# Hashed attention with experts: the later pairs' hash in four products, and the joining work two tiles back

## The chip, the cores and the metric

The kernel runs on one core of a Trainium2 chip. The metric is device time in microseconds of one execution, the median of the runs shown. Engines are called TensorE (PE), VectorE (DVE), ScalarE (ACT), GpSimd (POOL) and SyncE (SP, which here only issues DMAs). "PEld" is TensorE's weight load, "SPq" the queue of SyncE.

## The reference

Three layers follow each other; only the first is touched by the change.

```python
# attention: 2 batches, 8 heads, 768 tokens, 64 columns a head
q_bits = (q @ proj > 0); k_bits = (k @ proj > 0)          # proj: 64 x 6
q_bucket = sum(q_bits * 2 ** arange(6)); k_bucket likewise
scores = where(q_bucket == k_bucket, q @ k.T / 8, -1e9)   # token by token
attn = softmax(scores); x = attn @ v                      # f32
# mixture of 8 experts: each token goes to the expert of its largest x @ w_gate,
# is scaled by a gate weight and a sigmoid, runs through relu(x @ w1) @ w2
# last layer: elu(x @ w_in) @ w_out
```

Everything is f32. The kernel gets f32 accuracy from products of the type fp32r by splitting an operand into a high part (the rounded copy, "hi") and a low part (operand minus hi, "lo") and adding the products of the parts.

## The kernel before

**Attention** takes 16 heads as 8 pairs. A head has 6 tiles of 128 query tokens, so a pair has 12 tiles and there are 96 tiles, n = 0 to 95; "tile s of a pair" is n modulo 12. A head has two halves of 384 tokens, which have numbers m = 0 to 31 (three tiles each). One loop over n (lines 884 to 935) writes each engine's instructions in this order; every engine works through its own list in order and waits by semaphores. In the turn of tile n the list holds:

- `stage_M(n-1)`: VectorE takes the maximum of the scores of the tile before (L333), GpSimd makes from it a factor and a bias (L334, L335);
- `stage_A(n)`: sums on GpSimd that are due (L388);
- `early`: what an earlier turn has put off to here;
- `stage_T(n-3)`: TensorE turns the exponentials (six transposes, L362), ScalarE copies them out as hi (L364), VectorE makes lo (L365);
- `late[0]`, the first step of preparing the next pair;
- `stage_S(n)`: TensorE's scores, two column halves with two products each: L314 (q hi and lo with k hi), and L315, the masked product: q hi with k lo, and 38 mask rows that add a large negative number where the buckets differ;
- `stage_R` of a half, if due; `stage_V`, four products with v (L378);
- `stage_E(n-1)`: ScalarE's exponential (L342), which frees the score buffer (there are two);
- `stage_O` at the end of a half: ScalarE copies the output out; and `late[1]`, the second step of preparing.

**Preparing the next pair** is done in tiles 1, 2, 4, 5 (transposes of q and k, L203, copies and low parts) and 7, 8: the hash. `prep_Z(pr, j)` for j = 0, 1 (a column half of 384 tokens) issues six products (L229): q with a 128x128 matrix that holds proj for both heads, as hi x hi, hi x lo and lo x hi, and k likewise, into one PSUM buffer. In the following turn's `late[1]`, at its end, VectorE compares all 128 rows with 0 and multiplies with a column of amplitudes (`prep_Ze`, L245), which gives the rows of the mask for both heads. After j = 1, `restack` (L266) has SyncE move rows by DMA into the operands `kb` and `qb` of the next pair's heads: two for `kb` and one for `qb` for each head. The first pair's hash takes a way of its own (`first_Ze`). Transposes, hash and joins share three PSUM buffers of tag "t" (`ps_t`), which go round.

**The joining work.** Outputs leave PSUM as hi part and lo part products in 128 rows. `stage_O(m)`, at n = 3m+8, copies them to SBUF (L407), and a DMA shifts one half of the rows over (L408); the sum is put on a list with the tile 3m+11 at which `stage_A` runs it (L388). Copy and shift target are two tiles `o2` and `o1` of the pool `raw_p`, which has six large buffers of tag "w"; they are free again after the sum. From m = 26 on another way is taken. The same six buffers take the pieces of the experts' weights, 512 KB each: `load_piece` issues the first four at tiles 72, 75, 78 and 81 (L107), and they stay until attention is over. Once the second head of a pair has its half, `stage_R(m)`, here called the join, at n = 3m+13, multiplies the outputs of both heads with a matrix of the identity and the gates' weights (L454, six matmul records), which turns them to tokens by columns; its VectorE part (L462, L481) runs in the next turn's `early`. The output tiles `osb` have two buffers.

In the middle pairs the second head's halves are m = 2 and 3 (modulo 4), so joins stand in tiles 7 and 10 of the following pair; in pairs 3 and 7 the halves go by turns, m = 1 and 3 (modulo 4).

After attention come the gates' last part, the experts (a stretch in which TensorE is full) and the last layer; all wait for attention's end.

Of the kernel before, what the change touches and what calls it, by code (L numbers as in the profile page):

```python
# [8 lines left out]
F32 = mybir.dt.float32  # L9
F32R = mybir.dt.float32r  # L10
BF16 = mybir.dt.bfloat16
I32 = mybir.dt.int32
AF = mybir.ActivationFunctionType
ALU = mybir.AluOpType
# [5 lines left out]
BIG = float(2.0 ** 98)  # L20
NBITS = 6
# [4 lines left out]
def kernel(  # L26
# [15 lines left out]
    nc = tc.nc  # L42
    B, H, S, D = q.shape
# [5 lines left out]
    HALF = 3  # L49
    HC = HALF * 128  # L50
# [38 lines left out]
    raw_p = ctx.enter_context(tc.tile_pool(name="raw", bufs=6))  # L89
# [5 lines left out]
    PW = KD * F // 4  # L95
# [16 lines left out]
    ap2 = att.enter_context(tc.tile_pool(name="ap2", bufs=2))  # L112
    ops_s = ctx.enter_context(ExitStack())
    ap1 = ops_s.enter_context(tc.tile_pool(name="ap1", bufs=1))
    ps_s = att.enter_context(tc.tile_pool(name="ps_s", bufs=2, space=PSUM))
    ps_t = att.enter_context(tc.tile_pool(name="ps_t", bufs=3, space=PSUM))
# [45 lines left out]
        nc.gpsimd.memset(opnd[st, "kb"][64:96].bitcast(F32), -BIG)  # L162

    constant_rows(1)
    bdf, bdh, bdl = (ap1.tile([128, 2, 128], t, name="bd" + x) for x, t in (("f", F32), ("h", F32R), ("l", F32R)))
    nc.vector.memset(bdf, 0.0)
    for hh in range(2):
        rows = slice(64 * hh, 64 * hh + 64)
        src = pj[rows, None, :].to_broadcast([64, 2, NBITS])
        for nm, g0, c0, step in ((0, 32 * hh, 0, NBITS), (1, 64, NBITS * hh, 32)):  # L170
            dst = bdf[rows, nm, g0:g0 + 2 * step].rearrange("p (r c) -> p r c", r=2)[:, :, c0:c0 + NBITS]
            nc.scalar.activation(dst, src, AF.Copy)
    nc.scalar.activation(bdh, bdf, AF.Copy)
    nc.vector.tensor_tensor(bdl, bdf, bdh, ALU.subtract)
    bd = {nm: (bdh[:, i], bdl[:, i]) for i, nm in enumerate("qk")}
    amp = ap1.tile([128, 1], F32, name="amp")
    thr = ap1.tile([128, 1], F32, name="thr")
# [8 lines left out]
    for hh in range(2):  # L186
        p0 = 64 * hh
        rows, idc = slice(p0, p0 + 64), ident[p0:p0 + 64, None, p0:p0 + 64]
        nc.gpsimd.tensor_copy(rw[rows, :, hh, 0:D], idc.to_broadcast([64, H // 2, D]))
        nc.gpsimd.tensor_copy(rw_end[rows, :, 0:D], idc.to_broadcast([64, 2, D]))  # L190
    nc.gpsimd.memset(zt0, 0.0)

    hl = {}
# [26 lines left out]
    zt = {}  # L220
    zps = {}

    def prep_Zm(pr, j, nm):
        sl = slice(j * HC, (j + 1) * HC)
        if nm == "q":
            zps[pr, j] = ps_t.tile([128, HC], F32, tag="t", name="zps")
        hi, lo = hl[pr, nm]
        for i, (w, m) in enumerate(((bd[nm][0], hi), (bd[nm][0], lo), (bd[nm][1], hi))):
            nc.tensor.matmul(  # L229
                zps[pr, j], w, m[:, sl], start=(nm == "q" and i == 0), stop=(nm == "k" and i == 2)  # L230
            )
# [10 lines left out]
    def prep_Ze(pr, j):  # L242
        if j == 0:
            zt[pr] = ap2.tile([128, S], F32R, tag="z", name="z", bufs=1)
        nc.vector.tensor_scalar(  # L245
            zt[pr][:, j * HC:(j + 1) * HC], zps.pop((pr, j)), 0.0, amp[:, 0:1], ALU.is_gt, ALU.mult
        )

    def prep_Z(pr, j):
        prep_Zm(pr, j, "q")  # L250
        prep_Zm(pr, j, "k")

        def evac():
            prep_Ze(pr, j)
            if j == 1 and pr:
                restack(pr, "z")

        return (lambda: None), evac

    def restack(pr, what, heads=(0, 1)):  # L260
        for hh in heads:
            st = 2 * (pr % 2) + hh
            r0 = 64 * hh

            def cp(dst, p0, src, s0, n):
                nc.sync.dma_start(  # L266
                    opnd[st, dst][p0:p0 + n].bitcast(F32), src[s0:s0 + n].bitcast(F32)
                )

            if what == "q":  # L270
                hi, lo = hl[pr, "q"]
                cp("qa", 0, hi, r0, 64)
                cp("qa", 64, lo, r0, 64)
                cp("qb", 0, hi, r0, 64)
            elif what == "k":
                hi, lo = hl[pr, "k"]
                cp("ka", 0, hi, r0, 64)
                cp("ka", 64, hi, r0, 64)
                cp("kb", 0, lo, r0, 64)
            else:  # L280
                cp("kb", 64, zt[pr], (64, 96 + NBITS)[hh], NBITS)
                cp("kb", 96, zt[pr], (96, 64 + NBITS)[hh], NBITS)
                cp("qb", 64, zt[pr], 32 * hh, 2 * NBITS)

    vst = {}

# [103 lines left out]
    def stage_O(m):  # L390
        hd, hf = part_of(m)
        pr, hh = divmod(hd, 2)
        r0 = 64 * hh
        ps = ops.pop(m)
        if pr == NPAIR - 1 or hh == 0:
            t = ap2.tile([128, HC], F32, tag="osb", name="osb", bufs=2)
            osb.setdefault((pr, hf), []).append(t)
        if pr == NPAIR - 1:
            nc.scalar.activation(t, ps, AF.Copy)  # L399
            return  # L400
        t = osb[pr, hf][0][r0:r0 + 64]
        if m >= NM - 6:
            nc.scalar.activation(t, ps[0:64], AF.Copy)
            early.append(lambda: nc.vector.tensor_tensor(t, ps[64:128], t, ALU.add))
        else:
            w, u = (raw_p.tile([128, PW], F32, tag="w", name=x)[:, 0:HC] for x in ("o2", "o1"))
            nc.scalar.activation(w, ps, AF.Copy)  # L407
            nc.sync.dma_start(u[r0:r0 + 64], w[64 - r0:128 - r0])  # L408
            add.append((3 * m + 11, t, w[r0:r0 + 64], u[r0:r0 + 64]))

    rinv = {}
    sums_m = {}
# [24 lines left out]
    def stage_R(m):  # L437
        hd, hf = part_of(m)
        pr, hh = divmod(hd, 2)
        if hh == 0:  # L440
            return lambda: None
        b, pp = divmod(pr, H // 2)
        if pp == 0:
            xw[b, hf] = xlast if 2 * b + hf == NG - 1 else x_p.tile(
                [128, HALF, XC], F32, tag="xw", name="xw", bufs=NG - 1
            )
            nc.gpsimd.memset(xw[b, hf][:, :, DM:], 0.0)
            lg[b, hf] = x_p.tile([128, HALF, 2, 2 * E], F32, tag="lg", name="lg", bufs=NG)
        ts = osb.pop((pr, hf))
        ps = small_psum([128, HALF, 2, RW], False)  # L450
        for i, t in enumerate(ts):
            for a in range(HALF):
                o, w = (ps[:, a, i, :], rw_end[:, i, :]) if len(ts) == 2 else (ps[:, a], rw[:, pp])
                nc.tensor.matmul(o, t[:, a * 128:(a + 1) * 128], w, start=True, stop=True)  # L454
        return lambda: evac_R(pr, hf, ps)
# [427 lines left out]
    for n in range(NQ + 3):  # L883
        pr, s = divmod(n, 2 * NC)
        nx = pr + 1
        if NQ - 24 <= n < NQ - 12 and n % 3 == 0:
            load_piece((n - NQ + 24) // 3)
        if 1 <= n < NQ + 1:
            stage_M(n - 1)
        stage_A(n)  # L890
        both(early)
        early = []
        if 3 <= n < NQ + 3:
            m, part = divmod(n - 5, HALF)
            stage_T(n - 3, (lambda: stage_G2(m)) if m >= 0 and part == 0 else None)
        m, part = divmod(n - 4, HALF)
        if 0 <= m < NM and part == 0:
            stage_G(m)
        if late:
            late[0]()  # L900
        if n < NQ:
            stage_S(n)
        m, part = divmod(n - 13, HALF)
        if 0 <= m < NM - 3 and part == 0:
            early.append(stage_R(m))
        if n == NQ:
            stage_R(NM - 3)()
        m, part = divmod(n - 6, HALF)
        if 0 <= m < NM:
            stage_V(m, part)  # L910
        if 1 <= n < NQ + 1:
            stage_E(n - 1)
        if 0 <= m < NM and part == HALF - 1:
            stage_O(m)
        if late:
            late[1]()
            late = []
        for f, a in todo.pop(n, ()):
            f(*a)
        if n == NQ:  # L920
            ops_s.close()
            m2a = ctx.enter_context(tc.tile_pool(name="m2a", bufs=1, side="right", reuse_waits="tile"))
            split_piece(0, nc.gpsimd, nc.gpsimd, rest0)
            xt0 = [raw_p.tile([128, KD * CAP], F32R, tag="w", name="xt0") for _ in range(2)]
        if nx < NPAIR:
            if s % 3 and s < 9:
                late = prep(nx, s // 3 * 2 + s % 3 - 1)
            if s in v_at:
                i = v_at.index(s)
                early.append(lambda a=(nx, i // 3, i % 3): prep_V(*a))  # L930
            if nx + 1 < NPAIR:
                if s == 6:
                    load_pair(nx + 1, "qk")
                elif s == 11:
                    load_pair(nx + 1, "v")
# [423 lines left out]
```

## Time and profile before

| | |
|---|---|
| median of 3 runs | 722.96 us (722.31 to 724.34) |
| profiled execution | 723.3 us, span 721.5 us |
| granted clock, mean | 0.993 |
| TensorE busy | 704.7 us (98%) |
| VectorE busy | 553.6 us (77%) |
| ScalarE busy | 422.7 us (59%) |
| GpSimd busy | 206.0 us (29%) |

The profile is of one execution. The span runs from the first to the last instruction; the time of the execution is 1.8 us longer. A busy matmul is not one at its peak, since matmuls overlap and their ends are modelled: two matmuls with rows of 0.34 us each can follow each other at 0.17 us. Times in all rows count from the span's start.

### The profile page before, as it was taken

The numbers are of one execution on the slowest core, as the hardware profiler recorded it, in microseconds if no ns is written. First come the engines' busy times: TensorE is split into PE (matmuls) and PEld (weight loads), VectorE is DVE, ScalarE is ACT, GpSimd is POOL, SyncE is SP. The second block draws the span as 40 slices with busy tenths as digits, with TensorE's granted clock in tenths as the row PEclk, the third lists the DMA queues.
The fourth block names the chain that finished last, engine by engine and source line by source line (L and its number), as shares of the span: only waits on it lengthen the run. The fifth ranks groups of instructions, "written<-read, shape, count | busy, mean of one in ns | idle before, by whom it ended". The sixth has DMA issues, their size and how long they took to land.

```text
span 721.5 us, 12243 instructions
## 1 busy us (share of the span) xinstructions
PE 704.7 (98%) x4239; PEld 633.3 (88%) x4240; DVE 553.6 (77%) x1045; ACT 422.7 (59%) x843; POOL 206.0 (29%) x491
## 2 busy tenths in 40 slices
PE   6999999999999999999999999999999999999996
PEld 4899999999999988999999999788888888888885
DVE  5888988989898988788888887977688546934333
ACT  3887978879788875666666675444543224422221
POOL 7445454455545554112352241000000000002012
PEclk9899999999999999999999999999999999999999
DMA  8747576585773137987889786332122000001011
GB/s 192 181 104 172 163 184 173 129 213 137 167 218 98 76 105 224 291 251 222 260 241 251 203 230 191 103 102 84 63 88 87 31 0 2 1 0 59 0 59 61
DMA packets 108532, 97.69 MB, mean 135 GB/s; under 512 B 33416, under 2 KB 94472, under 8 KB 108464
## 3 DMA queue, kind: packets, MB, share of 16 engines
q1 hardware_dynamic: 106000, 90.44, 46.8%
q0 software_dynamic: 2304, 6.40, 2.4%
q8 instruction: 35, 0.57, 0.3%
q14 instruction: 33, 0.27, 0.1%
q10 hardware_dynamic: 160, 0.00, 0.0%
HBM read 64.15 MB, written 10.72 MB: 104 GB/s over the span
## 4 chain that ended last, share of the span: by engine, by line
PE 52%; issue 32%; DMA 7%; ACT 3%; DVE 2%; POOL 1%; SPq 1%; POOLq 0%; ACTq 0%; DVEq 0%
PE hps L1059 12%; PE o L378 8%; PE yps L1072 8%; PE t L362 7%; DMA out_dram<-part,tidt 5%; PE s L314 4%; PE s L315 4%; PE yps L1074 3%; PE zps L229 2%; PE sp L454 2%; ACT p L342 1%; PE prep L203 1%; PE xTp L1041 1%; DMA qb<-qhi 1%; DVE ptlo L365 1%
## 5 line engine op out<-in xcount | busy, mean ns | idle before, releaser
L365 DVE TENSOR_TENSOR ptlo<-t,pthi 128x384 fp32r<-128x384 f32 x192 | 100.1, 549 | 26.7 <-ACT pthi L364 24.5
L342 ACT ACTIVATE p<-s,bi,sc 128x768 f32<-128x768 f32 x96 | 96.1, 1001 | 21.4 <-POOL bi L335 20.0
L364 ACT ACTIVATE pthi<-t 128x384 fp32r<-128x384 f32 x192 | 84.9, 498 | 24.6 <-PE t L362 23.7
L765 DVE TENSOR_TENSOR wl<-wraw,wh 128x1024 fp32r<-128x1024 f32 x63 | 77.3, 1229 | 21.8 <-ACT wh L762 19.6
L333 DVE TENSOR_REDUCE nm<-s 128x1 f32<-128x768 f32 x96 | 91.0, 948 | 0.3 <-POOL vst L293 0.3
L1211 POOL DMA_INDIRECT out_dram<-part,tidt x12 | 11.5, 962 | 263.5 <-DVE part L1208 262.2
L1173 ACT ACTIVATE ee<-gps 128x512 f32<-128x512 f32 x48 | 28.7, 599 | 97.9 <-PE gps L1163 97.9
L1072 PE MATMUL yps<-h,wh 128*128 128x448 f32 x256 | 84.4, 380 | 0.0
L362 PE MATMUL t<-ident,p 128*128 128x128 f32 x576 | 80.5, 275 | 1.6 <-DVE qlo L212 1.6
L314 PE MATMUL s<-ka,qa 128*128 128x384 f32 x192 | 74.3, 387 | 3.0 <-ACT p L342 2.6
L1163 PE MATMUL gps<-x2h,vl 128*128 128x512 f32 x192 | 75.9, 395 | 0.0
L1193 PE MATMUL a<-vh,gh 128*128 128x512 f32 x192 | 75.6, 394 | 0.0
L1193 PE MATMUL a<-vh,gl 128*128 128x512 f32 x192 | 75.4, 393 | 0.0
L1163 PE MATMUL gps<-x2h,vh 128*128 128x512 f32 x192 | 75.3, 392 | 0.0
L1163 PE MATMUL gps<-x2l,vh 128*128 128x512 f32 x192 | 75.2, 392 | 0.0
L1193 PE MATMUL a<-vl,gh 128*128 128x512 f32 x192 | 74.9, 390 | 0.0
L362 PEld LDWEIGHTS t<-ident,p 128*128 128x128 f32 x576 | 68.5, 142 | 5.2 <-DVE qlo L212 2.0
L1174 DVE TENSOR_SCALAR ee<-ee 128x512 f32<-128x512 f32 x48 | 20.4, 425 | 66.2 <-ACT ee L1173 66.2
L1176 ACT ACTIVATE gh<-ee 128x512 fp32r<-128x512 f32 x48 | 30.4, 634 | 69.2 <-DVE ee L1175 69.2
L378 PE MATMUL o<-pthi,vst 128*128 128x384 f32 x192 | 67.1, 349 | 0.8 <-ACT osb L399 0.6
L315 PE MATMUL s<-kb,qb 102*128 102x384 f32 x192 | 66.2, 345 | 0.8 <-DMA qb<-qhi 0.8
L762 ACT ACTIVATE wh<-wraw 128x1024 fp32r<-128x1024 f32 x63 | 66.1, 1052 | 0.2 <-DMA wraw<-in_moe_w_dram 0.2
(204 smaller groups left out, 1772.1 us busy)
## 6 DMA issues: line engine op xcount, KB each, us to landing
wraw<-in_moe_w_dram SPq DMA_DIRECT2D x64, 512.0 KB
w<-in_moe_w_in_dram SPq DMA_DIRECT2D x16, 512.0 KB
w<-in_moe_w_out_dram SPq DMA_DIRECT2D x16, 512.0 KB
ka<-khi SPq DMA_DIRECT2D x30, 192.0 KB
xs_d<-zt SPq DMA_DIRECT2D x8, 528.0 KB
xs<-xs_d SPq DMA_DIRECT2D x8, 528.0 KB
raw_q<-in_q_dram SPq DMA_DIRECT2D x16, 192.0 KB
raw_k<-in_k_dram SPq DMA_DIRECT2D x16, 192.0 KB
```

Source lines behind the costliest of these rows:

```text
L314: nc.tensor.matmul(ps[:, j, 0:HC], opnd[st, "qa"][:, cb], opnd[st, "ka"][:, sl], start=True, stop=False)
L315: nc.tensor.matmul(ps[:, j, 0:HC], opnd[st, "qb"][0:64 + MROWS, cb], opnd[st, "kb"][0:64 + MROWS, sl], start=False, stop=True,)
L333: nc.vector.tensor_reduce(nm, sps[n][:, :, 0:HC], AX.XY, ALU.max, negate=True)
L342: nc.scalar.activation(p.rearrange("p (a b) -> p a b", a=2), sps.pop(n)[:, :, 0:HC], AF.Exp, bias=bi, scale=sc, accum_out=sums[hd][:, c:c ...
L362: nc.tensor.transpose(ps[:, a, :], p[:, kt * 128:(kt + 1) * 128], ident)
L364: nc.scalar.activation(ho, ps, AF.Copy)
L365: nc.vector.tensor_tensor(lo[:, HALF * g:HALF * (g + 1), i * 128:(i + 1) * 128], ps, ho, ALU.subtract)
L378: nc.tensor.matmul(ops[m], vst[hd][:, kt, :], t[:, kt, :], start=(kt == 0 and x == 0), stop=(kt == NC - 1 and x == 1))
L1059: nc.tensor.matmul(ps, w[:, dc, fs], x[:, dc], start=(i == 0), stop=(i == len(terms) - 1))
L1072: nc.tensor.matmul(ps, wh[:, f], h[:, :, f], start=(f == 0), stop=last)
L1163: nc.tensor.matmul(ps, w[:, dc], x[:, dc, th * TC:(th + 1) * TC], start=(dc == 0 and i == 0), stop=(dc == KD - 1 and i == 2),)
L1193: nc.tensor.matmul(ps, x[:, cs], w, start=(fb in first_fb and i == 0), stop=(fb in last_fb and i == 2))
```

## The change

For the later seven pairs the hash is laid out in another way. A new matrix `zw` holds in columns 0 to 63 the hi part of proj at the places of all rows that are wanted, and in columns 64 to 127 the negative lo part. Four products (q hi, q lo, k hi, k lo with it) put into rows 0 to 63 of PSUM the product with hi and into rows 64 to 127 minus the product with lo. ScalarE copies the lower 64 rows to SBUF at once; in the next turn's `early`, so behind the next maximum and ahead of that turn's low parts, VectorE compares the upper rows with the copy, and GpSimd multiplies the bits with a column of amplitudes in place. `restack` follows there, with new row numbers. The matrix is made at the start with two fills, four small ScalarE copies and two GpSimd operations; its f32 form and that of the old matrix lie in large buffers of `raw_p`. The old matrix stays for the first pair.

The sums of the halves m = 0 to 23 are due at 3m+13 instead of 3m+11, the joins of these halves at 3m+15 instead of 3m+13; from m = 24 on both stay. `osb` has three buffers instead of two. `raw_p` keeps its six.

```diff
--- before.py
+++ after.py
@@ -162,8 +162,16 @@
         nc.gpsimd.memset(opnd[st, "kb"][64:96].bitcast(F32), -BIG)
 
     constant_rows(1)
-    bdf, bdh, bdl = (ap1.tile([128, 2, 128], t, name="bd" + x) for x, t in (("f", F32), ("h", F32R), ("l", F32R)))
+    bdf, zwf = (
+        raw_p.tile([128, PW], F32, tag="w", name=x)[:, 0:2 * n].rearrange("p (i c) -> p i c", i=2)
+        for x, n in (("bdf", 128), ("zwf", 64))
+    )
+    bdh, bdl, zw = (ap1.tile([128, 2, 128], F32R, name=x) for x in ("bdh", "bdl", "zw"))
+    zamp = ap1.tile([64, 1], F32, name="zamp")
     nc.vector.memset(bdf, 0.0)
+    nc.vector.memset(zwf, 0.0)
+    for p0, n, a in ((0, 32, 1.0), (32, 32, -BIG), (32, 2 * NBITS, 2.0 * BIG)):
+        nc.vector.memset(zamp[p0:p0 + n], a)
     for hh in range(2):
         rows = slice(64 * hh, 64 * hh + 64)
         src = pj[rows, None, :].to_broadcast([64, 2, NBITS])
@@ -172,6 +180,12 @@
             nc.scalar.activation(dst, src, AF.Copy)
     nc.scalar.activation(bdh, bdf, AF.Copy)
     nc.vector.tensor_tensor(bdl, bdf, bdh, ALU.subtract)
+    for hh in range(2):
+        rows = slice(64 * hh, 64 * hh + 64)
+        src = pj[rows, None, :].to_broadcast([64, 2, NBITS])
+        for i, c0, step in ((0, 2 * NBITS * hh, NBITS), (1, 32 + NBITS * hh, 2 * NBITS)):
+            dst = zwf[rows, i, c0:c0 + 2 * step].rearrange("p (r c) -> p r c", r=2)[:, :, 0:NBITS]
+            nc.scalar.activation(dst, src, AF.Copy)
     bd = {nm: (bdh[:, i], bdl[:, i]) for i, nm in enumerate("qk")}
     amp = ap1.tile([128, 1], F32, name="amp")
     thr = ap1.tile([128, 1], F32, name="thr")
@@ -188,6 +202,8 @@
         rows, idc = slice(p0, p0 + 64), ident[p0:p0 + 64, None, p0:p0 + 64]
         nc.gpsimd.tensor_copy(rw[rows, :, hh, 0:D], idc.to_broadcast([64, H // 2, D]))
         nc.gpsimd.tensor_copy(rw_end[rows, :, 0:D], idc.to_broadcast([64, 2, D]))
+    nc.gpsimd.tensor_copy(zw[:, :, 0:64], zwf)
+    nc.gpsimd.tensor_tensor(zw[:, :, 64:128], zw[:, :, 0:64], zwf, ALU.subtract)
     nc.gpsimd.memset(zt0, 0.0)
 
     hl = {}
@@ -247,15 +263,25 @@
         )
 
     def prep_Z(pr, j):
-        prep_Zm(pr, j, "q")
-        prep_Zm(pr, j, "k")
+        sl = slice(j * HC, (j + 1) * HC)
+        if j == 0:
+            zt[pr] = ap2.tile([128, S], F32R, tag="z", name="z", bufs=1)
+        ps = ps_t.tile([128, HC], F32, tag="t", name="zps")
+        for i, nm in enumerate("qk"):
+            for x, t in enumerate(hl[pr, nm]):
+                nc.tensor.matmul(ps, zw[:, i], t[:, sl], start=(i == 0 and x == 0), stop=(i == 1 and x == 1))
+        low = zt[pr][64:128, sl].bitcast(F32)
+        nc.scalar.activation(low, ps[64:128], AF.Copy)
+        z = zt[pr][0:64, sl]
 
         def evac():
-            prep_Ze(pr, j)
-            if j == 1 and pr:
+            nc.vector.tensor_tensor(z, ps[0:64], low, ALU.is_gt)
+            nc.gpsimd.tensor_scalar(z, z, zamp, None, ALU.mult)
+            if j == 1:
                 restack(pr, "z")
 
-        return (lambda: None), evac
+        early.append(evac)
+        return []
 
     def restack(pr, what, heads=(0, 1)):
         for hh in heads:
@@ -278,9 +304,10 @@
                 cp("ka", 64, hi, r0, 64)
                 cp("kb", 0, lo, r0, 64)
             else:
-                cp("kb", 64, zt[pr], (64, 96 + NBITS)[hh], NBITS)
-                cp("kb", 96, zt[pr], (96, 64 + NBITS)[hh], NBITS)
-                cp("qb", 64, zt[pr], 32 * hh, 2 * NBITS)
+                k0, k1, q0 = (32 + NBITS * hh, 32 + NBITS * (2 + hh), 2 * NBITS * hh) if pr else (96 + NBITS, 64 + NBITS, 32)
+                cp("kb", 64, zt[pr], k0, NBITS)
+                cp("kb", 96, zt[pr], k1, NBITS)
+                cp("qb", 64, zt[pr], q0, 2 * NBITS)
 
     vst = {}
 
@@ -393,7 +420,7 @@
         r0 = 64 * hh
         ps = ops.pop(m)
         if pr == NPAIR - 1 or hh == 0:
-            t = ap2.tile([128, HC], F32, tag="osb", name="osb", bufs=2)
+            t = ap2.tile([128, HC], F32, tag="osb", name="osb", bufs=3)
             osb.setdefault((pr, hf), []).append(t)
         if pr == NPAIR - 1:
             nc.scalar.activation(t, ps, AF.Copy)
@@ -406,7 +433,7 @@
             w, u = (raw_p.tile([128, PW], F32, tag="w", name=x)[:, 0:HC] for x in ("o2", "o1"))
             nc.scalar.activation(w, ps, AF.Copy)
             nc.sync.dma_start(u[r0:r0 + 64], w[64 - r0:128 - r0])
-            add.append((3 * m + 11, t, w[r0:r0 + 64], u[r0:r0 + 64]))
+            add.append((3 * m + (13 if m < NM - 8 else 11), t, w[r0:r0 + 64], u[r0:r0 + 64]))
 
     rinv = {}
     sums_m = {}
@@ -900,9 +927,9 @@
             late[0]()
         if n < NQ:
             stage_S(n)
-        m, part = divmod(n - 13, HALF)
-        if 0 <= m < NM - 3 and part == 0:
-            early.append(stage_R(m))
+        for m in range(NM - 3):
+            if n == 3 * m + (15 if m < NM - 8 else 13):
+                early.append(stage_R(m))
         if n == NQ:
             stage_R(NM - 3)()
         m, part = divmod(n - 6, HALF)
```

## Rows read from the trace of the kernel before

**Rows 1.** The page: busy us, share and instructions by engine; clock in 40 slices
```profile
PE 704.7 (98%) x4239; PEld 633.3 (88%) x4240; DVE 553.6 (77%) x1045; ACT 422.7 (59%) x843; POOL 206.0 (29%) x491
...
PEclk9899999999999999999999999999999999999999
```
**Rows 2.** Stretches: from:to, length, busy by engine (count), clock, DMA share, GB/s
```profile
62.00:92.50 30.50, 30.49 (x206) 29.53 (x205) 26.78 (x52) 25.18 (x56) 14.08 (x47) 1.00 0.67 170
```
**Rows 3.** Waits, 20 to 260 us: who <- whom: total us, times, longest
```profile
...
DVE ptlo L365 <- ACT pthi L364: 24.5, 43, 1.4
ACT pthi L364 <- PE t L362: 23.7, 39, 1.5
...
PEld s L314 <- ACT p L342: 4.6, 17, 0.6
```
**Rows 4.** The chain of waits around tile 19: start, us, what
```profile
60.50 0.82 PE sp L454 x6
...
62.02 1.04 PE zps L229 x6
63.06 0.66 PE t L362 x6
```
**Rows 5.** Timeline of TensorE (start, us, what): score products of tiles 10, 11, 19, 23, 24
```profile
38.44 0.42 PE L314 MATMUL s<-ka,qa 128*128 128x384 f32 x1
...
41.08 0.44 PE L314 MATMUL s<-ka,qa 128*128 128x384 f32 x1 [0.33 <-ACT p L342]
...
59.52 0.44 PE L314 MATMUL s<-ka,qa 128*128 128x384 f32 x1
...
71.55 0.42 PE L314 MATMUL s<-ka,qa 128*128 128x384 f32 x1
...
73.61 0.42 PE L314 MATMUL s<-ka,qa 128*128 128x384 f32 x1
73.87 0.34 PE L315 MATMUL s<-kb,qb 102*128 102x384 f32 x1
```
**Rows 6.** Timeline of ScalarE: small copies, q's cast, an output's copy
```profile
4.51 0.31 ACT L172 ACTIVATE bdf<-pj 64x12 f32<-64x12 f32 x2 [0.72 <-DMA pj<-in_proj_dram]
...
6.21 0.87 ACT L208 ACTIVATE qhi<-prep 128x384 fp32r<-128x384 f32 x2 [0.94 <-PE prep L203]
...
73.24 0.50 ACT L407 ACTIVATE o<-o 128x384 f32<-128x384 f32 x1
```
**Rows 7.** Timeline of VectorE in tile 20
```profile
61.99 0.55 DVE L481 TENSOR_TENSOR xw<-sp,ri 128x384 f32<-128x384 f32 x1
63.95 0.56 DVE L365 TENSOR_TENSOR ptlo<-t,pthi 128x384 fp32r<-128x384 f32 x1 [1.41 <-ACT pthi L364]
...
64.95 0.61 DVE L245 TENSOR_SCALAR z<-zps,amp 128x384 fp32r<-128x384 f32 x1
```
**Rows 8.** Timeline of GpSimd: a cast at the start, the sum of half 23
```profile
9.04 0.82 POOL L600 CAST ka<-khi 64x768 fp32r<-64x768 f32 x1 [1.54 <-ACT khi L208]
...
215.89 1.00 POOL L388 TENSOR_TENSOR osb<-o,o 64x384 f32<-64x384 f32 x1
```
**Rows 9.** Timeline of SyncE's queue in pair 1: a half's shift, a mask row
```profile
67.44 0.74 SPq L408 DMA_DIRECT2D o<-o  x1
...
70.25 0.74 SPq L266 DMA_DIRECT2D qb<-z  x1
```
**Rows 10.** Timeline of SyncE's queue: the third and fourth piece of weights
```profile
210.97 0.54 SPq L107 DMA_DIRECT2D wraw<-in_moe_w_dram  x1
...
219.36 0.59 SPq L107 DMA_DIRECT2D wraw<-in_moe_w_dram  x1
```
**Rows 11.** Waits of SyncE's queue, 196 to 232 us
```profile
SPq L107 <- POOL bi L335: 0.6, 1, 0.6
```
**Rows 12.** Timeline of TensorE: tile 84
```profile
226.98 0.42 PE L314 MATMUL s<-ka,qa 128*128 128x384 f32 x1
```
**Rows 13.** Stretches: the early one at half clock
```profile
18.20:25.00 6.80, 5.38 (x21) 5.19 (x22) 5.46 (x9) 5.76 (x12) 2.65 (x10) 0.50 0.79 178
```

## The prediction

> **What bounds the kernel now.** I read the engines' busy shares first [rows 1]: TensorE is busy 98% of the span at full granted clock, VectorE 77%. A busy TensorE need not be the limit, so the stretches come next [rows 2]. In the pair of heads from 62.0 to 92.5 us TensorE is busy 30.49 of 30.50 us, VectorE 26.78, ScalarE 25.18, GpSimd 14.08. The waits over all tiles of attention [rows 3] show who waits: ScalarE 23.7 us for TensorE's transposes, VectorE 24.5 us for ScalarE, and TensorE only 4.6 us in 17 pieces, for the exponential that frees a score buffer. So in attention TensorE's own instructions set the end, with a thin rim of waits. The chain of waits [rows 4] says the same: join, hash and transposes stand in it back to back. The tiles' lengths come from the timeline of the score products [rows 5]: a plain tile takes 73.61 - 71.55 = 2.06 us, and each join or hash in a tile comes on top.
>
> **The products.** Six hash products take 1.04 us on the chain [rows 4], 0.173 us each. Four instead of six in 14 halves (seven later pairs) remove 28: 28 x 0.173 = **-4.85 us**. The columns and the operand type stay, so I take the same pitch. The Trainium skill (TensorE: Matmul & The Clock Gate, "Back-to-back issue gap") gives columns / 2.4 + 2.5 ns for a warm array; an estimate from it is 162.5 ns for 384 columns and -4.55 us. The row is 7% slower; the row is used.
>
> **The hash's new copy, compare and multiply.** Before, one VectorE operation of 0.61 us stood at the end of the next tile, ahead of the following maximum; now ScalarE copies 64 partitions of the product, VectorE compares behind the next maximum, GpSimd multiplies. The copy lies between the two small copies (0.31 us for two of 64x12 [rows 6]) and 0.50 us for 128x384 [rows 6]; I take 0.5. ScalarE stands idle for TensorE in a hash tile, so the copy is hidden. Queued behind it are the next tile's two casts; they need the transposes of 0.66 us that TensorE starts only after the hash, so they come at most 0.1 us later, and VectorE's low parts behind them have 1.41 us of idle time in that place [rows 7]. The compare is a two-operand operation of 384 columns from PSUM, 0.55 us [rows 7] instead of 0.61, and fills that idle time. If the cover failed, compare and copy would cost up to 1.05 us in 14 places; I keep nothing of that, for the nearest rows show the idle time.
> So the maximum after a hash tile starts about 0.6 us earlier. That pays once where nothing hides it: in the first pair (no join yet) the tile from 38.44 to 41.08 took 2.64 us [rows 5] with a wait for the exponential at its end, 0.58 over a plain one: **-0.55** (bounds 0 and -0.58). In later pairs a join lay in that tile. GpSimd's multiply lies between 0 and 1.01 us (two inputs, 64x384), nearest 0.41 (half of a 64x768 cast of 0.82 us) [rows 8]; it follows the compare, GpSimd is busy 14 of 30.5 us, and the rows for the next pair are complete some 2 us earlier than now: no cost.
>
> **The joins two tiles back.** Twelve joins of 0.82 us [rows 4], their work on VectorE (0.55 us of it the scaling of x [rows 7]) and the 24 sums before them move; none goes away. What changes is the cover. From tile 7 of a pair to tile 9, from 10 to the next pair's tile 0: no longer beside the hash. Their VectorE work falls into tile 10, where it did into 11, and into tile 1, which has TensorE's transposes of q as cover. I expect a few small waits to go (the 4.6 us of [rows 3] less the 0.58: I let **-0.3** go, bounds -1.5 and 0) and VectorE's lag after tile 1 to add **+0.2** (0 to 0.6).
> Two things get tight. First, the join now asks for the PSUM buffer that the second hash holds. From the hash's end to the join TensorE has transposes (0.66) and four score products (0.70 at the pitch above), 1.36 us; copy, compare and handoffs need 0.5 + 0.55 + 0.25 = 1.30. **+0.3** for six pairs (0 to 1.2).
> Second, the next pair's mask rows. From tile 19 to tile 24, 73.61 - 59.52 = 14.09 us become 14.09 - 0.82 - 0.70 = 12.57, so tile 24's first masked product moves from 73.87 to 72.35 us in this trace's time. SyncE's queue is then the late one: it ends the half's shift at 67.44 + 0.74 = 68.18 us [rows 9]; mask rows then follow at once, and the third of head 0 is issued two times 0.8 us later, at 69.9. From issue to landing lies between 0.74 us (the issue itself) and 3.62 us (70.25 to 73.87, where no wait is recorded); I take the middle, 2.2: 72.1, just in time. **+0.2** for six pairs (0 to 6.8).
>
> **A wait that the diff does not show.** Each half's shift takes two of the six large buffers from its copy (tile 3m+8) to its sum, now at 3m+13 instead of 3m+11; the expert weights' first four pieces take one each at tiles 72, 75, 78 and 81. At tile 78 two pieces and halves 22 and 23 hold all six, so the third piece waits for half 22's sum in tile 79, and half 24's shift, behind it in SyncE's queue, for half 23's sum in tile 82. Now these pieces go at 210.97 and 219.36 us [rows 10], and such a DMA already shows a wait for GpSimd [rows 11]. Queued behind: the last pair's k rows (early enough), the fourth piece and the last pair's mask rows, for which TensorE waits in tile 84. Half 23's sum starts at 215.89 and takes 1.00 us [rows 8]; two tiles of 2.06 + 0.69 us later it ends at 222.4. Then shift 0.5, piece 0.6, two mask issues 1.6 on the queue, and 2.2 to landing: 227.3. Tile 84 started at 226.98 [rows 12]; without one join and with two shorter hashes it starts at 225.46, its masked product at 225.7. **+1.6** (0, if buffers come free otherwise, to 3.0).
>
> **The start.** Four tiny ScalarE copies more (0.62 us by [rows 6]) lie in 0.94 us of idle time before q's cast; GpSimd's two operations before a wait for k. No cost; 0.3 if the cover is gone.
>
> **Sum.** -4.85 - 0.55 - 0.3 + 0.2 + 0.3 + 0.2 + 1.6 = -3.4 us against the profiled execution's 723.3 (span 721.5 and 1.8 around it): 719.9. The median of the runs, 722.96, is 0.3 lower; for it I forecast **719.6**. Behind attention everything waits on its end, so the shift carries through.
>
> **The rivals.**
> *No shortage of buffers* (chance 0.22): the 1.6 us don't appear, 718.0. For it: only the program's order says so, no row. Against: the count above.
> *Mask rows late in every pair* (0.08), the side on which it gets slower: the price is 6 times the lateness, and it decides from 0.6 us each (landing 3.1 us after issue) between gain and loss. At the bound of 3.62 us each pair waits 73.5 - 72.35 = 1.15 us, 6.9 in all instead of 0.2: 726.3. For it: SyncE's queue is full there and the 1.5 us of slack are what the change spends. Against: transfers of few bytes.
> *The clock falls in the wait of tile 84* (0.08): early on, after idle stretches of TensorE, the granted clock was 0.50 for 6.80 us (level 1.2 GHz, else 2.4) [rows 13]. Half of that, 3.4 us, on top: 723.0. Against: dense work on both sides of one wait. The Trainium skill (same page, "What's actually happening") says that throttled is the default and activity lifts it; the stretch at 0.50 agrees.
> *VectorE and ScalarE set the pace* (0.10): VectorE has 26.8 of 29.8 us then, and half of the freed product time comes back as waits for the exponential: 722.0. For it: the 17 waits. Against: in the hash tile VectorE waits and is not waited for [rows 7].
> The forecast has 0.50, the unnamed rest 0.02.
>
> **How the numbers follow.** Likeliest case: 718.2 to 721.4, from the small bounds together. The range **716.4 to 722.6** takes in the case without shortage with more waits gone, and the slow pace; outside are late rows and half of the clock case. About 0.3%, 2.2 us, is what a measurement can tell here: faster means under 720.8. That holds for 0.80 of the forecast, all of the first rival and 0.3 of the last: **0.66**; slower, over 725.1, the late rows and little else: **0.08**; same **0.26**.
>
> **What will show it.** Hash runs of 0.69 us with four products; the first pair's tile 10 at 2.06; no masked product at a pair's start with a wait; the third piece some 4 us later after tile 77 than now, and TensorE's one wait in tile 84. Wrong it is if pairs stay above 30.0 us, or if waits over 0.5 us stand before a pair's first masked product.

## The result, and the profile after

The changed kernel takes **730.61 us** (median of 6 runs, 728.93 to 731.3) against 722.96 us before on the same chip: 1.0101 times as long, interval 1.0089 to 1.0113. It is slower by 7.7 us, where 719.6 us and a gain of 3.4 us were forecast. The profiled execution took 731.3 us, span 729.5.

The page after, busy time, share and instructions by engine, and the clock in 40 slices (compare [rows 1]):

```profile
PE 707.6 (97%) x4211; PEld 631.7 (87%) x4212; DVE 557.2 (76%) x1049; ACT 429.3 (59%) x861; POOL 219.7 (30%) x507
...
PEclk8899999999999999999999999999999999999999
```

There are 28 matmuls fewer, as forecast, and yet the span is 8.0 us longer. The stretches of the changed kernel, a middle pair (tiles 31 to 42) and the neighbourhood of tile 84 (columns as in [rows 2]):

```profile
89.77:121.04 31.27, 30.48 (x200) 28.81 (x201) 26.92 (x51) 26.15 (x59) 17.16 (x48) 1.00 0.68 166
...
231.00:237.00 6.00, 4.46 (x20) 4.45 (x21) 2.77 (x6) 2.10 (x6) 1.92 (x8) 0.72 0.15 32
```

In [rows 2] TensorE had 0.01 us of holes in a pair; now it has 0.79, and GpSimd has 3 us more work (2.5 of them the two multiplies of the hash). The second line is a stretch with the granted clock at 0.72. Waits of the changed kernel from 20 to 260 us (who <- whom: total us, times, longest):

```profile
ACT p L369 <- POOL bi L362: 17.4, 35, 1.0
...
PEld s L341 <- ACT p L369: 8.5, 25, 0.8
...
DVE z L278 <- ACT z L274: 6.6, 13, 0.7
...
PEld s L342 <- DMA kb<-z: 2.2, 1, 2.2
PE s L342 <- DMA qb<-z: 2.0, 1, 2.0
...
PE sp L481 <- DVE z L278: 1.8, 4, 0.6
```

TensorE's wait for the exponential is 8.5 us in 25 pieces where it was 4.6 in 17 [rows 3], and the exponential itself waits for GpSimd's bias. Two lines are new: one masked product waits 2 us for mask rows, and joins wait for the compare of the hash.

**Where it happens** is read from the length of each tile, from the start of its first score product to the next one's in TensorE's timeline. The rows "tile 5" to "tile 0" are means over tiles 24 to 47 and 60 to 71 (the pair with a gate's products is left out); the row of a pair takes in all four pairs from tile 24 to 71; the last two rows are single stretches. "Hash only" and "sums back" are the first and third experiment below.

| us | before | after | hash only | sums back |
|---|---|---|---|---|
| tile 5 | 2.41 | 2.61 | 2.41 | 2.41 |
| tile 6 | 2.34 | 2.49 | 2.34 | 2.34 |
| tile 7 | 3.95 | 2.79 | 3.60 | 2.79 |
| tile 8 | 3.11 | 2.82 | 2.77 | 2.76 |
| tile 9 | 2.08 | 3.55 | 2.07 | 3.11 |
| tile 10 | 2.88 | 2.07 | 2.89 | 2.07 |
| tile 11 | 2.07 | 2.67 | 2.07 | 2.10 |
| tile 0 | 2.13 | 2.90 | 2.12 | 2.88 |
| a pair, mean of tiles 24 to 71 | 30.57 | 31.55 | 29.86 | 30.10 |
| tile 84 | 2.36 | 6.68 | 2.36 | 2.89 |
| tile 0's start to tile 94's | 239.62 | 246.01 | 233.71 | 234.26 |

Tiles 5, 6, 9 and 11 have grown, and tile 84 by 4.3 us. (Joins have moved from tiles 7 and 10 to 9 and 0, which explains part of tile 9 and all of tile 0.) What delays tile 11 is seen from the start of a tile 10, here tile 46 (130.06 to 132.13 us), in GpSimd's timeline of the changed kernel (start, us, what); then come the exponential on ScalarE and the score product on TensorE that follow:

```profile
130.45 1.02 POOL L415 TENSOR_TENSOR osb<-o,o 64x384 f32<-64x384 f32 x1
131.55 0.39 POOL L494 TENSOR_TENSOR lg<-lg,lp 128x96 f32<-128x96 f32 x1
131.88 0.29 POOL L319 CAST vst<-raw_v 128x128 fp32r<-128x128 f32 x1
132.25 0.47 POOL L320 TENSOR_TENSOR vst<-raw_v,vst 128x128 fp32r<-128x128 f32 x1
132.80 0.23 POOL L444 TENSOR_SCALAR sm<-sums 128x3 f32<-128x3 f32 x1
133.12 0.22 POOL L361 TENSOR_SCALAR sc<-nm 128x1 f32<-128x1 f32 x1
133.42 0.19 POOL L362 TENSOR_TENSOR bi<-sc,nm 128x1 f32<-128x1 f32 x1
```
```profile
133.65 0.99 ACT L369 ACTIVATE p<-s,bi,sc 128x768 f32<-128x768 f32 x1 [0.69 <-POOL bi L362]
```
```profile
134.79 0.44 PE L341 MATMUL s<-ka,qa 128*128 128x384 f32 x1 [0.34 <-ACT p L369]
```

Here `sc` and `bi` are the factor and the bias of the next exponential, and `sm` is a small operation once a half: it makes of the sums of exponentials what VectorE's reciprocal reads. The moved sum (L415), the add of the gates' logits (L494), the preparation of v (L319, L320: hi and lo part) and `sm` follow each other with holes of 0.1 us at most for 2.6 us in a tile of 2.07, and the next tile's `sc` and `bi` come straight behind. So the exponential is 0.69 us late and TensorE waits. In the kernel before, around the same tile (129.66 to 132.55 us), the next sum comes behind `bi`, and the exponential does not wait (GpSimd, then ScalarE):

```profile
131.06 0.29 POOL L292 CAST vst<-raw_v 128x128 fp32r<-128x128 f32 x1
...
131.99 0.24 POOL L417 TENSOR_SCALAR sm<-sums 128x3 f32<-128x3 f32 x1
...
132.66 0.19 POOL L335 TENSOR_TENSOR bi<-sc,nm 128x1 f32<-128x1 f32 x1
132.81 1.01 POOL L388 TENSOR_TENSOR osb<-o,o 64x384 f32<-64x384 f32 x1
```
```profile
133.26 1.00 ACT L342 ACTIVATE p<-s,bi,sc 128x768 f32<-128x768 f32 x1
```

Before, the sums stood in tiles 2, 5, 8 and 11; v stood (and stands) in 4, 6, 7, 9, 10 and 0, and `sm` in 1, 4, 7 and 10. Two tiles back the sums stand in 1, 4, 7 and 10: all of them beside `sm`, three of four beside v.

### The profile page after: what moved, and what is told of

It is laid out like the page before. It is cut to its first block, busy times and chain, and to the rows that moved or that the text cites. A ratio compares the mean times of both kernels' runs of the same rounds, so it can differ in the third digit from the quotient of the medians.

```text
span 729.5 us, 12241 instructions
## 1 busy us (share of the span) xinstructions
PE 707.6 (97%) x4211; PEld 631.7 (87%) x4212; DVE 557.2 (76%) x1049; ACT 429.3 (59%) x861; POOL 219.7 (30%) x507
## 4 chain that ended last, share of the span: by engine, by line
issue 36%; PE 35%; ACT 8%; POOL 8%; DMA 6%; DVE 5%; SPq 1%; POOLq 0%; DVEq 0%; ACTq 0%
PE hps L1086 10%; PE yps L1099 7%; DMA out_dram<-part,tidt 4%; PE o L405 3%; PE yps L1101 3%; ACT p L369 3%; PE t L389 3%; ACT pthi L391 2%; POOL osb L415 2%; PE s L341 2%; PE sp L481 2%; PE s L342 2%; DVE ptlo L392 1%; POOL vst L320 1%; POOL sc L361 1%
## 5 line engine op out<-in xcount | busy, mean ns | idle before, releaser
L369 ACT ACTIVATE p<-s,bi,sc 128x768 f32<-128x768 f32 x96 | 96.1, 1001 | 22.7 <-POOL bi L362 22.1
```

The costliest lines, as they stand in the source:

```text
L369: nc.scalar.activation(p.rearrange("p (a b) -> p a b", a=2), sps.pop(n)[:, :, 0:HC], AF.Exp, bias=bi, scale=sc, accum_out=sums[hd][:, c:c ...
```

## The experiments

Theory A was this reading: the joining work costs, by GpSimd's queue and by the large buffers, and the hash is a gain. Theory B was that the hash's own chain of ScalarE, VectorE and GpSimd costs. Each result below is the median, its ratio to the kernel before beside it on the same chip, and the ratio's interval. Chips differ a little, so versions that ran on different chips are compared by these ratios. In the cuts of code `...` stands for what is left out, and words behind # are not in the kernels.

**1. The hash alone**
```diff
# from the changed kernel
- add.append((3 * m + (13 if m < NM - 8 else 11), t, ...
+ add.append((3 * m + 11, t, ...
-   if n == 3 * m + (15 if m < NM - 8 else 13):     # joins
+   if n == 3 * m + 13:
- name="osb", bufs=3
+ name="osb", bufs=2
```


> Only the hash is changed: sums on GpSimd and joins stand where they stood in the kernel before (3m+11, 3m+13). Theory A (the loss is the joining work's: its sums now fall on GpSimd beside the v casts and hold back the biases of the next exponentials, its joins wait for the PSUM buffer of the second hash, and its large buffers come free too late for tile 84): the products give back 0.35 us for each of 12 half-pairs and the first pair about 0.6, start +0.75, so 718.5 to 720.5 us, faster than before. Theory B (the loss is the hash's own: ScalarE's copy, then VectorE's compare, then GpSimd's multiply of 1.26 us stand in tiles 7 to 9 and delay exponentials there): pairs stay at 31 us or longer, 727 to 731 us.

Measured: 718.82 us, 0.995 (0.9931 to 0.997). Faster by 0.5%, clear of the interval; A holds, B falls. In its profile TensorE has hardly a hole left in the middle of attention, 159.72 of 160 us:

```profile
60.00:220.00 160.00, 159.72 (x1077) 154.35 (x1077) 145.37 (x293) 139.86 (x314) 95.11 (x270) 1.00 0.71 175
```

**2. The joining work alone** (the other half: sums, joins and `osb` as in the changed kernel, put on the kernel before, its hash left as it was)

> Only the joining work is moved (sums at 3m+13, joins at 3m+15, third sum buffer), the hash is that of the kernel before. Theory A: the whole loss without the gain of the products, 0.95 us of GpSimd's queue in each of six pairs, tile 84 some 4 us late, and less of the PSUM wait since the old hash frees its buffer one VectorE operation after its products: 729 to 734 us. Theory B: the move is near neutral, 720 to 724 us.

Measured: 733.51 us, 1.0141 (1.0115 to 1.0167); pairs 31.98 us against 30.57, tile 84 6.65 us. The loss is there without any of the hash.

**3. The sums back, the joins still two tiles back**
```diff
# from the changed kernel
- add.append((3 * m + (13 if m < NM - 8 else 11), t, ...
+ add.append((3 * m + 11, t, ...
```


> The changed kernel with its GpSimd sums back at 3m+11, joins still at 3m+15. Theory A: GpSimd's collisions (0.95 us in each of six pairs) and the late pieces of tile 84 (about 4 us) go together, the wait of the joins for the second hash's buffer (0.55 us in each pair) stays: 720 to 722.5 us. Theory A without the GpSimd part (only the large buffers were late): about 726 us. Theory B: 728 to 731 us.

Measured: 718.93 us, 0.995 (0.9931 to 0.9969). One number in one line takes back some 11 us (1.0101 against 0.995 of the kernel before). That is below the 720 to 722.5 us that A gave, for the joins' wait for the second hash's buffer is smaller than the 0.55 us a pair assumed there. The move of the joins is nearly neutral: pairs 30.10 us against 29.86 with the hash alone, since a pair's two joins show with 3.11 - 2.07 = 1.04 and 2.88 - 2.12 = 0.76 us in tiles 9 and 0, where they showed with 0.81 and 0.82 in tiles 7 and 10; against that, tiles 12 to 23 carry one join less (28.99 us against 29.74).

**4. v out of the sums' tiles**
```diff
# from the changed kernel
- v_at = (3, 5, 6, 8, 9, 11)
+ v_at = (1, 2, 4, 5, 10, 11)
```
(`v_at` holds the turns that put the work off; it runs one tile later.)

> The changed kernel with the v preparation in tiles 2, 3, 5, 6, 11 and 0 of a pair in place of 4, 6, 7, 9, 10 and 0, so that no v cast stands in a tile with a moved sum; large buffers as in the changed kernel. If the collision of the sums with the v casts costs 0.95 us a pair: 724 to 726 us, tile 84 still over 6 us long. If the sums themselves (1.0 us of GpSimd in tiles that also take the reciprocals' part and the logits) cost that: 729 to 731 us, no change.

Measured: 726.42 us, 1.0054 (1.0035 to 1.0073). Pairs fall from 31.55 to 30.00 us, all of the loss in the pairs; tile 84 stays, at 7.00 us. The total is a little over the 724 to 726 us expected and gains less than the pairs because the first pair lost 3.2 us (33.62 from tile 0 to tile 12 against 30.46): in its tiles 1 to 6 GpSimd prepares that pair's own v too, and tile 3 takes 5.43 us against 2.56.

**5. The late sums alone, where weights are loaded**
```diff
# from the changed kernel
- add.append((3 * m + (13 if m < NM - 8 else 11), t, ...
+ add.append((3 * m + (13 if 20 <= m < NM - 8 else 11), t, ...
```


> The changed kernel with the sums of halves 20 to 23 alone at 3m+13, all others at 3m+11. Theory C (two costs, in two places): the late halves keep large buffers from the third and fourth piece, tile 84 takes 6.5 to 7 us in place of 2.9, pairs 30.1 us as with all sums back: 721.5 to 723.5 us. Rival D (what tile 84 shows is only the backlog that GpSimd's queue has gathered by then): tile 84 below 3.5 us, 718.5 to 719.5 us.

Measured: 724.33 us, 1.0025 (1.0014 to 1.0036), a little over the span of what I expected. Pairs are 30.08 us; tile 84 takes 4.98 us, not 6.5 to 7: so C is right on the place, and the rest of tile 84 is another cost (experiment 9).

**6. Both mended**
```diff
# from the changed kernel
- add.append((3 * m + (13 if m < NM - 8 else 11), t, ...
+ add.append((3 * m + (13 if m < 20 else 11), t, ...
- if s in v_at: i = v_at.index(s)
+ vs = v_at if nx == 1 else (1, 2, 4, 5, 10, 11)
+ if s in vs: i = vs.index(s)
```


> The changed kernel, joins and most sums at their late places, with two mends: v preparation in tiles 2, 3, 5, 6, 11, 0 from the second pair on (the first pair as in the changed kernel), and the sums of halves 20 to 23 at 3m+11. Theory C: pairs 30.0 us, tile 84 below 3.2 us, 717.5 to 720 us, so that nothing of the loss is left. Rival D: the late sums still cost in their tiles, over 722 us.

Measured: 718.64 us, 0.9951 (0.9933 to 0.9968). Late sums cost nothing when GpSimd has room in their tiles and the weights' buffers are free in time. With 1 and 3 it is one of three versions at 0.995 of the kernel before; the three can't be told apart. Experiments 7 and 10 beat the kernel before too, by less.

**7. The multiply on VectorE**
```diff
# from experiment 1
- nc.gpsimd.tensor_scalar(z, z, zamp, None, ALU.mult)
+ nc.vector.tensor_scalar(z, z, zamp, None, ALU.mult)
```


> The hash alone (sums at 3m+11, joins at 3m+13) with the multiply of the hash bits on VectorE in place of GpSimd. If GpSimd's 1.26 us in tiles 8 and 9 is hidden work: 718 to 720 us as with the multiply on GpSimd. If it is a cost: up to 1 us a pair less, 713 to 716 us. If VectorE, busy for 0.9 of the middle pairs, cannot take the 0.4 to 0.6 us: 720 to 724 us.

Measured: 720.71 us, 0.9981 (0.9969 to 0.9992); pairs 30.09 us against 29.86. Nothing is gained, so GpSimd's 1.26 us were hidden in experiment 1; VectorE takes the work, at the lower edge of the third case, with at most a small loss: the interval of the ratio just touches that of experiment 1.

**8. One large buffer for a sum in place of two**
```diff
# from the changed kernel
- w, u = (raw_p.tile([128, PW], F32, tag="w", name=x)[:, 0:HC] for x in ("o2", "o1"))
+ wu = raw_p.tile([128, PW], F32, tag="w", name="o21")
+ w, u = wu[:, 0:HC], wu[:, HC:2 * HC]
```


> The changed kernel with the two parts of a half's sum in one large buffer in place of two; all places in the order of work as in the changed kernel. Theory C: the pieces find free buffers, tile 84 falls from 6.7 to about 2.9 us, the granted clock stays at 1.00 from 231 to 237 us, pairs stay at 31.5 us: 726 to 727.5 us. Rival E (the late pieces are only carried along by VectorE and GpSimd being late, buffers are not short): 729 to 731 us.

Measured: 726.84 us, 1.0058 (1.0044 to 1.0072); tile 84 2.91 us, pairs 31.56, clock 1.00 from 222 to 243 us. With free buffers the whole loss of tile 84 goes, 3.8 us, though the pairs are as late as in the changed kernel: C holds, E falls.

**9. TensorE kept busy in tile 84**
```diff
# from the changed kernel
+ if n == 84:
+     keep_warm(12, True)     # twelve products
  if n < NQ:
      stage_S(n)
```


> The changed kernel with twelve products of 384 columns, whose result nothing reads, put on TensorE ahead of tile 84's score products, where it waits 2.0 us for the masked product. If the granted clock of 0.72 from 231 to 237 us is a cost of its own that follows from the idle engine: clock 1.00 there, tile 84 about 5.0 us in place of 6.7, 728.5 to 729.5 us. If the clock falls for another reason, or the pieces alone make tile 84 so long: 730 to 731.5 us.

Measured: 729.84 us, 1.0097 (1.0082 to 1.0111), which lies between the two cases and overlaps the changed kernel's interval, so the time alone doesn't show it. The timelines of TensorE do: first the changed kernel, then the kernel with the products, then experiment 5.

```profile
230.10 0.44 PE L341 MATMUL s<-ka,qa 128*128 128x384 f32 x1 [0.15 <-ACT p L369]
232.54 0.66 PE L342 MATMUL s<-kb,qb 102*128 102x384 f32 x1 [2.00 <-DMA qb<-z]
233.00 0.52 PE L341 MATMUL s<-ka,qa 128*128 128x384 f32 x1
```
```profile
229.69 2.11 PE L617 MATMUL warm<-ones_b 128*128 128x384 bf16 x12
231.51 0.47 PE L341 MATMUL s<-ka,qa 128*128 128x384 f32 x1
232.26 0.41 PE L342 MATMUL s<-kb,qb 102*128 102x384 f32 x1 [0.29 <-DMA qb<-z]
232.52 0.34 PE L341 MATMUL s<-ka,qa 128*128 128x384 f32 x1
```
```profile
222.43 0.44 PE L341 MATMUL s<-ka,qa 128*128 128x384 f32 x1 [0.18 <-ACT p L369]
224.72 0.41 PE L342 MATMUL s<-kb,qb 102*128 102x384 f32 x1 [1.84 <-DMA qb<-z]
224.97 0.34 PE L341 MATMUL s<-ka,qa 128*128 128x384 f32 x1
```

In the first, products behind the wait take 0.52 us at the lower clock, in the others 0.34. Tiles 83 and 84 together take 9.37 us in the changed kernel and 7.68 with the warm products, where the mask row came 0.2 us sooner after tile 83's start. From the end of the wait to tile 85 it is 4.24 us against 2.72: 1.5 us belong to the clock in that execution. In experiment 5's profiled execution a wait nearly as long (1.84 us) left the clock at 1.00:

```profile
222.00:226.00 4.00, 1.98 (x13) 1.51 (x12) 2.20 (x5) 2.60 (x7) 1.79 (x5) 1.00 0.38 109
```

So a wait of this length doesn't bring the fall every time. Whether the clock fell in the other ten executions of experiment 5 is not shown: their mean clock is 0.990 to 0.992 where the profiled one had 0.994, and their spans are longer (721.6 to 725.3 us against 721.4), but experiment 8's profiled execution has a mean of 0.992 without a fall in tile 84.

The traces of other experiments tell the wait from GpSimd's lag. In experiment 4 the pairs are short, tile 83 takes 2.31 us and tile 84 begins without a wait for an exponential; yet the clock falls behind the wait for the mask row (a row of TensorE, then the stretch):

```profile
227.69 0.62 PE L342 MATMUL s<-kb,qb 102*128 102x384 f32 x1 [2.27 <-DMA qb<-z]
```
```profile
226.00:231.00 5.00, 3.31 (x12) 3.34 (x13) 2.46 (x6) 2.32 (x5) 2.32 (x10) 0.67 0.21 44
```

Experiment 12 shows the same (tile 83 at 2.31 us, a wait of 2.72, clock 0.76 from 228 to 235 us). In experiment 8 the lag is there (tile 83 at 2.68 us) and the wait is not, and the clock stays at 1.00. So in these traces the wait brings the fall, and the lag alone does not. Experiments 2 and 11 have it too, behind waits of 1.89 and 2.40 us (clock 0.72 from 234 to 240 and from 226 to 232 us).

**10. v on the sums' tiles, sums back** (the reverse of 4)
```diff
# from experiment 3
- if s in v_at: i = v_at.index(s)
+ vs = v_at if nx == 1 else (1, 4, 5, 7, 10, 11)
+ if s in vs: i = vs.index(s)
```


> The reverse of the kernel with v moved: sums back at 3m+11 (tiles 2, 5, 8, 11), joins at 3m+15, and from the second pair on the v preparation put on the sums' tiles (2, 5, 6, 8, 11, 0). If it is the meeting of a sum (1.0 us) and a v cast with its subtraction (0.75 us) in one tile of GpSimd's queue that costs, wherever the sum stands: pairs 30.5 to 31.3 us in place of 30.1, 720.5 to 726 us; less than in the changed kernel, since the sums' tiles do not take the reciprocals' part here. If the late place of the sums is what costs: pairs 30.1 us, 718 to 720 us.

Measured: 720.74 us, 0.9966 (0.9952 to 0.998), but pairs of 30.03 us, none longer than with the sums back. The median is just in the first range, but the pairs say that this case failed: a sum and v in one tile are not enough. The pairs fit the other case, the late place of the sums; but that place alone isn't enough either, for experiment 4 has it, with pairs of 30.00 us. Two things are missing here against the changed kernel: `sm` in the same tile (and in tile 10 the logits' add), and a late start of the sum, which begins 0.49 and 0.61 us into tiles 2 and 5 of a pair here (seen in tiles 38 and 41) and 1.19 and 1.33 us into tiles 4 and 7 there (tiles 40 and 43). Experiment 11 tries the first.

**11. `sm` one tile later**
```diff
# from the changed kernel
- m, part = divmod(n - 5, HALF)     # reciprocal, in stage_T
+ m, part = divmod(n - (6 if n < 77 else 5), HALF)
- m, part = divmod(n - 4, HALF)     # sm
+ m, part = divmod(n - (5 if n < 76 else 4), HALF)
```


> The changed kernel with the small GpSimd operation sm of every half (0.23 us, tiles 4, 7, 10, 1) and the reciprocal that reads it one tile later, so that sums, v casts and sm no longer stand in the same tile. Theory F (a tile's work on GpSimd must fit into the tile: 1.0 for the sum, 0.75 for v, 0.23 for sm and 0.4 for the two bias operations are 2.4 us with gaps near 2.6, over the 2.4 of tile 4): tile 5 and tile 6 lose their 0.3 and 0.2 us, tile 11 keeps most of its 0.6, pairs 30.9 to 31.2 us in place of 31.55, 727.5 to 729.5 us. Rival G (only the meeting of sum and v matters): pairs 31.5, 730 to 731 us.

Measured: 725.14 us, 1.0022 (1.0012 to 1.0032); pairs 30.50 us. A GpSimd operation of 0.23 us, moved by one tile, gives back 1.05 us a pair, more than F had it and against G. (VectorE's reciprocal had to move with it.) GpSimd's timeline of that kernel around the same tile 10 shows how:

```profile
126.87 1.01 POOL L415 TENSOR_TENSOR osb<-o,o 64x384 f32<-64x384 f32 x1
127.96 0.39 POOL L494 TENSOR_TENSOR lg<-lg,lp 128x96 f32<-128x96 f32 x1
128.29 0.29 POOL L319 CAST vst<-raw_v 128x128 fp32r<-128x128 f32 x1
128.66 0.46 POOL L320 TENSOR_TENSOR vst<-raw_v,vst 128x128 fp32r<-128x128 f32 x1
129.09 0.21 POOL L361 TENSOR_SCALAR sc<-nm 128x1 f32<-128x1 f32 x1
129.39 0.19 POOL L362 TENSOR_TENSOR bi<-sc,nm 128x1 f32<-128x1 f32 x1
129.66 0.24 POOL L444 TENSOR_SCALAR sm<-sums 128x3 f32<-128x3 f32 x1
```

`sm` now stands behind `bi`. From the sum's start to `sc` it is 2.22 us here and 2.67 in the changed kernel. `sm` was the last thing ahead of the bias that the exponential waits for, in three tiles of a pair that had no room left.

**12. One v preparation out of tile 10**
```diff
# from the changed kernel
- v_at = (3, 5, 6, 8, 9, 11)
+ v_at = (3, 5, 6, 8, 10, 11)
```


> The changed kernel with one v preparation of six moved, from tile 10 to tile 11 of each pair. Theory F: tile 10 holds a sum, v, sm, the logits' add (0.4 to 0.7) and the bias operations, 2.8 to 3.1 us of GpSimd in a tile of 2.15; without v it is 2.1 to 2.3 and tile 11 falls from 2.72 to 2.1 to 2.3 us, others unchanged: pairs 31.0 to 31.2 us, 727.5 to 729 us. Rival G: tile 11 falls the same, but tile 9 and tile 5 too, pairs below 30.7 us, 725 to 727 us. If tile 10 is not the place: 730 to 731 us.

Measured: 727.58 us, 1.0052 (1.0034 to 1.0069). Tile 11 falls from 2.67 to 2.10 us and no other tile; pairs 30.93 us. What is too much for GpSimd in tile 10 is paid in tile 11 and nowhere else, as F has it; G had tiles 5 and 9 fall too.

## Why the prediction was wrong

The sum by the starts of tiles 0 and 94 in the profiled executions: the hash -5.9 us (experiment 1 against before), the joins +0.6 (3 against 1), the sums +11.7 (after against 3); together +6.4. The medians, each against the kernel before beside it, say -3.7, +0.1 and +11.3, together +7.7. The two accounts differ because the tiles leave out what lies before tile 0 and behind tile 94, and because a profiled execution is not the median one (experiment 1's is the fastest of its five).

The sign that I had named for being wrong, pairs above 30.0 us, came: 31.55.

- **The failed step** is "Twelve joins ... and the 24 sums before them move; none goes away. What changes is the cover": I went on to VectorE's and TensorE's cover and never placed the sums in GpSimd's queue. For GpSimd I had only "busy 14 of 30.5 us" as a reason for no cost, and that was said of the multiply. That average hid that three tiles of a pair (4, 7 and 10) were to get 2.4 to 3 us of work in tiles of 2.1 to 2.8, ahead of the bias for the next exponential. Price: no term in my sum; 1.45 us a pair, 8.2 us over tiles 12 to 83 (188.04 against 179.83 us). Shown by experiments 3, 4, 6, 11 and 12.
- **The buffer shortage** was right in place and mechanism. In experiment 5, at full clock, tile 84 grows by 4.98 - 2.89 = 2.1 us, within the 0 to 3.0 around my 1.6. In the changed kernel it is 3.8, clock included. SyncE's queue there:

```profile
218.69 0.37 SPq L107 DMA_DIRECT2D wraw<-in_moe_w_dram  x1
...
227.32 0.59 SPq L107 DMA_DIRECT2D wraw<-in_moe_w_dram  x1
227.95 1.52 SPq L292 DMA_DIRECT2D kb<-z  x2
229.52 0.75 SPq L292 DMA_DIRECT2D qb<-z  x1
```

  Third and fourth piece go 7.7 and 8.0 us later than in [rows 10]; counted from the start of tile 77 in each kernel (211.03 and 207.80 us) it is 4.5 and 4.7, where I had some 4 for the third. The mask row that is waited for takes 3.0 us from issue to the masked product, where I took 2.2 of 0.74 to 3.62.
- **The clock rival** (0.08) came in on top of it, as it was priced: 1.5 us of the 3.8 in the profiled execution, under half of the 3.4 I gave.
- **Products**: 0.69 us a run forecast; tiles 7 and 8 lose 0.35 and 0.34 us (experiment 1 against before), two of six products at 0.173. Right.
- **The hash's chain**: hidden, as costed, though the multiply took 1.26 us, over my upper bound of 1.01, which was a sum of two inputs of the same shape. GpSimd's timeline of experiment 1:

```profile
152.50 1.26 POOL L279 TENSOR_SCALAR z<-z,zamp 64x384 fp32r<-64x384 f32 x1
```

  The first pair's tile 10 fell to 2.40 us, 0.24 less and not 0.55 (2.06 was forecast). By the trace the hash's -5.9 us are more than the 5.4 forecast because tile 4 took 2.05 us (experiment 1) against 2.76: from 22.7 to 25.5 us the granted clock was 0.84 there and 0.58 before. It is scatter, for with the same start experiment 8 has 2.95. By the medians it is -3.7, with an interval from -2.2 to -5.0.
- **The PSUM buffer** that the second hash holds: with the sums back, the join in tile 9 shows 0.28 us more than the one in tile 0, with all mended 0.2 (tile 9 3.02 us), for which no row names the buffer, so the cause is argued; I had 0.05 a pair, 0.2 at most. In the changed kernel GpSimd's lag reaches it: exponential late, ScalarE's copy late, compare late. VectorE, then TensorE, in tile 9:

```profile
127.20 0.55 DVE L278 TENSOR_TENSOR z<-zps,z 64x384 fp32r<-64x384 f32 x1 [0.70 <-ACT z L274]
```
```profile
127.90 1.05 PE L481 MATMUL sp<-rw,osb 128*128 128x160 f32 x6 [0.35 <-DVE z L278]
```

- **Small waits and VectorE's lag after tile 1**: with the sums back TensorE waits 4.6 us for the exponential in 16 pieces, as long as in [rows 3], and tiles 1 to 4 are as before; 0 for -0.3 and 0 for +0.2.
- **Mask rows at pair starts**: at the six starts before tile 84 no masked product waits; 0 for +0.2. **VectorE and ScalarE set the pace**: no; in experiment 1 TensorE has no holes.
- **The start**: tile 0 began at 11.59 us against 10.84, but in eleven more profiled kernels with this start (experiments 1 and 3 to 12) it began at 10.49 to 11.43, median 10.95. No cost that stands out of the scatter.

Without the move of the sums my other terms give -4.85 - 0.55 - 0.3 + 0.2 + 0.3 + 0.2 = -5.0 us, and experiment 3 measured -3.6 (0.995 of 722.55, interval -2.2 to -5.0): at the interval's edge.

What stays open: why the clock stayed at 1.00 behind the 1.84 us wait of experiment 5; and whether experiment 10 is slower than experiment 3, with pairs of equal length (0.9966 against 0.995 of the kernel before, with intervals that overlap).

## What to carry to other kernels

An engine that is idle half of the time can still be full in one tile: where work is moved between turns of a loop, add up, for every engine, what stands in the new turn ahead of the operation that the critical engine waits for, and hold it against that turn's length. The last small operation ahead of such a one is the cheapest to move (0.23 us moved gave 1.05 us a pair). A wait for a buffer that runs through a queue of DMAs can be counted from the program's order and a few rows; here that gave the place, and the size within 0.5 us at full clock (1.6 against 2.1).

## What was not expected of the hardware

GpSimd's multiply of 64x384 with a column of factors takes 1.26 us, longer than its sum of two tensors of that shape at 1.01. The granted clock fell after single waits of TensorE of 1.89 to 2.72 us in the middle of dense work, in five profiled executions (to 0.72 from 231 to 237 us in the changed kernel, after 2.0 us), and stayed at 1.00 behind a wait of 1.84 us in another.
